# An attention and SwiGLU kernel: the first set's seam in two halves, and a new order of the prologue

## The chip, the cores and the metric

The kernel runs on one core of a Trainium2 chip. The core has TensorE (PE, matmuls into PSUM), VectorE (DVE), ScalarE (ACT), GpSimd (POOL) and SyncE (SP, which issues most DMAs); each works through its own list of instructions in order, and semaphores tie the lists together. The metric is the device time in microseconds (us), as a median of runs.

## The reference

Two blocks follow each other. The first is an attention with 32 inducing points, for 4 batches of 12416 rows of 128 channels: the inducing points attend to the rows, and then the rows to the result h.

```python
def mab(q, kv):
    s = scale * (q @ kv.transpose(0, 2, 1))
    s = s - s.max(-1, keepdims=True)
    a = np.exp(s)
    a /= a.sum(-1, keepdims=True) + 1e-09
    return a @ kv
h = mab(I, x)
return mab(x, h)
```

The second is a feed-forward block on all 49664 rows, with d_ff = 1536:

```python
xn = x / rms * rms_g
g = xn @ w_gate
silu = g * (1.0 / (1.0 + np.exp(-g)))
val = xn @ w_val
return silu * val @ w_out
```

The weights come in as 64-bit numbers, and the kernel makes 32-bit ones of them.

## The kernel before, in words

**Tiling.** A batch's rows are cut into seven sets: five of 2048 rows, one of 1920, one of 256. A set of the large kind has four units (quarters); a unit is 512 tokens wide, and the feed-forward runs for each unit over 12 slots of 128 of the 1536 hidden columns. Since the second attention's output is a combination of the 32 rows of h, the weights w_gate and w_val are multiplied by h once for each batch; the results are the stacks sg and sv. A slot is then a gate matmul (L745) of sg with the unit's moving tile a, SiLU on ScalarE (L753), a value matmul (L756) with sv, their product on DVE (L762), and the matmul with w_out (L682, L703, L705), plain or in three parts for which ScalarE, DVE and POOL prepare factors (L727 to L737). Order and PSUM banks of this long stage stand in lists in the code: which PSUM bank each call takes (`banks`), which work tile (`workers`), at which slot each other step goes (`places`).

**The seam of a set** makes moving tiles out of the second attention's scores. `scores2` multiplies the set's rows, channels first (xT), with h turned over (hT), and DVE turns the result (L440); DVE takes the maximum over the 32 points (L444) and subtracts it (L448), ScalarE takes the exponential (L455). Then `seam` (L499): turn (L511), a matmul with the Gram matrix of h (L515), product and turn (L521, L522), sum and mean square with a floor (L526, L527), the power -1/2 on POOL (L532), its product with the weights (L536), turn (L540), and a split into an upper half of rounded numbers (L548 on DVE for the first set) and the remainder (L549). The normalisation of the softmax falls out, since the RMS norm divides by it again. For the first unit of the first set, `spread` brings upper half and remainder of one quarter to all 128 partitions with two matmuls (L571), and ScalarE copies the result (L574); for the others, `gather` does it with four DMAs from SP (L561).

**The prologue** is everything that comes before the first slot of the first batch: x is loaded (L137, L141), turned by TensorE (L820) and copied by ScalarE and DVE (L826), scored against the inducing points (L341, L832), with maxima by group of sets (L838 to L849), exponentials (L857), turns (L376), sums (L865), sums folded (L400), each group's sum weighed (L878) and turned into hT (L884, L889), and hT is scaled into hg (L425). Beside it the weights are converted chunk by chunk: load (L217), exponent (L257, L237), mantissa (L270, then L239 on ScalarE or L241 on DVE), sign (L279), remainder (L285), product on POOL (L287), and for w_gate and w_val a store to DRAM (L229). A chunk is named by its matrix (0 gate, 1 value, 2 out) and its number: p01 is the exponent of chunk 1 of w_gate. The matmul of a chunk with hg is L483, its copy L484, and L488 takes the remainder for the lower 64 partitions.

**What sets the order.** There is no scheduler: instructions go to the engines in the order in which the code issues them. In the prologue that order is the string ORDER (L793), 170 names that are called one after the other: t transposes, a and v copies by ScalarE and DVE, s scores, m evictions, e exponentials, r turns, h sums, by weighing, p, P, u, U, g, l the weight steps, st and low the stacks, w20 a run of 20 matmuls whose results nobody reads (L191). PSUM banks of the prologue are taken in turn from five (`bank`, L297), work tiles by the digits of `works` (L295). The sequence of SP's DMAs follows from the same order.

Of the kernel before, what the change touches and what calls it, by code (L numbers as in the profile page):

```python
# [18 lines left out]
P = 128  # L19
R = 4  # L20
# [3 lines left out]
def kernel(  # L24
# [269 lines left out]

    NB, turn, turns, works, factors = 5, [0], [], [int(c) for c in "01202121"], []  # L295

    def bank():  # L297
        if turns:
            n = turns.pop(0)
        else:  # L300
            n = turn[0] % NB
            turn[0] += 1
        return ps_gv.tile([P, 512], F32, name="gv", tag=f"gv{n}")
# [5 lines left out]
    def attention(b, load_next):  # L309
# [27 lines left out]
        def scores(s, lhsT, nq, n):  # L337
            w = n * m
            ps = bank()
            for q in range(nq):  # L340
                nc.tensor.matmul(ps[ts(q, m), 0:w], lhsT, xT[b, s][:, ts(q, w)], start=True, stop=True)  # L341
            return ps[0:nq * m, 0:w]
# [94 lines left out]

        def scores2(s, ps=None):
            ps = ps or scores(s, st["hT"][:, 0:m], quarters[s], per2[s])
            nc.vector.transpose(out=sc[b][rows2[s], cols2[s]], in_=ps)  # L440
# [112 lines left out]
    def gather(b, u):  # L553
# [6 lines left out]
        for k, half in enumerate((hi, lo, hi, lo)):  # L560
            nc.sync.dma_start(out=a[ts(k, m), 0:w].bitcast(F32), in_=half[ts(q, m), 0:w].bitcast(F32))  # L561

    def spread(b, u):

        s, q = units[u]
        w = per2[s] * m
        hi, lo = split_of[b, s]
        assert not q and not flowing
        ps = bank()
        for k, half in enumerate((hi, lo)):  # L570
            nc.tensor.matmul(ps[:, 0:w], sel[:, k, :, :].rearrange("p k m -> p (k m)"), half[:, 0:w],  # L571
                             start=not k, stop=bool(k))
        a = moving[b, u] = astk.tile([P, 512], F32R, name="a")
        nc.scalar.copy(out=a[:, 0:w], in_=ps[:, 0:w])  # L574

# [212 lines left out]
    def join(i, c):  # L788
# [4 lines left out]
    ORDER = """  # L793
        open w3 t00 a00 t02 v02 t01 t03 v03 t11 v11 a01 t13 s0 t10 t12 v13 a12 t22 a10 m0 t20 a22 t23 a23 t21 v21 s1
        a20 s2 t30 m1 p00 P00 a30 m2 t31 a31 t33 own0 a33 g00 mB0 nb0 t32 t43 v32 a43 u00 t41 a41 t40 t42 e1 e0 v42 e2
        s3 t51 v40 t50 s4 m3 a50 a51 t53 t52 t60 r0 ls0 h0 r2 U00 r1 l00 a53 a52 a60 s5 m4 own1 m5 s6 mB1 nb1 m6 e3
        own2 p20 e4 h1 u20 r3 mB2 nb2 e6 p10 e5 r4 r6 ls1 ls2 h2 h3 h4 least r5 share shared fold by0 u10 Uv10 h5 h6
        P20 by1 by2 turn_h g20 p01 hT sc2 P10 g10 U20 l10 T2 gram rmax P01 sub exp2 silu l20 ta w11 sq g01 u01 st1 tz
        sum st0 low1 low0 p11 u11 P11 root Uv01 l01 ap tb split w20 spread w3 gather1 gather2 U11
    """  # L800

    def first():
# [87 lines left out]

        def scores2():
            at["scores2"] = f["scores"](0, st["hT"][:, 0:m], R, per2[0])

        def table():
            tiny = small.tile([P, 1], F32, name="tiny")
            S.activation(tiny[:], ones, AF.Silu)

        do = {"open": f["open_"], "least": least_of, "share": shares, "shared": shared,
              "fold": f["fold_l"], "turn_h": turn_h, "hT": copy_h, "sc2": scores2, "gram": f["square_h"],
              "T2": lambda: f["scores2"](0, at["scores2"]), "rmax": lambda: f["row_max"](0), "sub": lambda: f["sub_max"](0),  # L900
              "exp2": lambda: f["exp2"](0, 1), "silu": table, "spread": lambda: spread(0, 0), "lows": lambda: None}
        for n in range(1, 40):
# [18 lines left out]
        for i in range(2):  # L921
            do[f"st{i}"] = lambda i=i: f["stack_of"](i, 0)
            do[f"low{i}"] = lambda i=i: f["stack_low"](i, 0)
        for name, step in zip(("ta", "sq", "tz", "sum", "root", "ap", "tb", "split"), seam(0, 0)):
            do[name] = step
        for u in (1, 2):
# [309 lines left out]
```

## Time and profile before

| | |
|---|---|
| median of 3 runs | 1576.13 us (1575.78 to 1576.47) |
| the profiled execution's own time | 1576.26 us |
| its span, first to last instruction | 1574.4 us |
| granted TensorE clock | 0.999 |
| busy: PE, DVE, ACT, POOL | 1560.7, 1463.9, 1300.1, 1432.8 us |
| first gate matmul (L745) starts | 51.03 us |

The profile is of one execution. Its page shows busy times, the chain of work that ended last, and the costliest groups of instructions. A line of the chain has start, length, engine, what is written and the line. A line of the timeline has start, length, engine, line, operation, tiles and size, and in brackets how long the engine stood idle before it and what ended that. A line of the busy times by stretch has the stretch, its length, the busy us (and instructions) of PE, PE's weight loads, DVE, ACT and POOL, the granted clock, the busy share of the DMA engines and GB/s. A line of the groups by shape has line, engine, operation, tiles, sizes and count, then the sum in us and the mean in ns, and then idle time before.

### The profile page before, as it was taken

How to read it: one execution, taken by the hardware profiler on the slowest of the kernel's cores; microseconds unless marked ns; L12 is line 12 of the kernel's file. 1: busy time of each engine (PE TensorE's matmuls, PEld its weight loads, DVE VectorE, ACT ScalarE, POOL GpSimd, SP SyncE). 2: the span in 40 equal slices, each digit the busy share in tenths (PEclk: the TensorE clock that was granted, in tenths of full speed). 3: DMA queues.
4: the chain of work that ended last, by engine and by line, in shares of the span. 5: the costliest groups of instructions: out<-in, count | busy, mean ns of one | idle time of the engine just before them, and what ended most of it. 6: DMA issues, size and time to landing. Idle time of an engine off the chain costs nothing.

```text
span 1574.4 us, 26146 instructions
## 1 busy us (share of the span) xinstructions
PE 1560.7 (99%) x7152; PEld 1109.1 (70%) x7152; DVE 1463.9 (93%) x2539; ACT 1300.1 (83%) x2496; POOL 1432.8 (91%) x1159
## 2 busy tenths in 40 slices
PE   8999999999999999999999999999999999999998
PEld 6556667767776667776777667776677777777777
DVE  7899999999999998999999999898999999999997
ACT  5677888788888889887988888978798888888886
POOL 1379999999999999999999999899989999999998
PEclk9999999999999999999999999999999999999999
DMA  6445525335453141634444323353222111122221
GB/s 260 104 79 92 100 53 118 79 76 88 68 90 67 33 94 34 134 70 95 71 76 83 54 58 75 73 117 73 47 39 38 37 34 36 33 36 38 40 39 27
DMA packets 389331, 112.58 MB, mean 72 GB/s; under 512 B 365088, under 2 KB 369728, under 8 KB 386624
## 3 DMA queue, kind: packets, MB, share of 16 engines
q1 hardware_dynamic: 388592, 110.83, 35.4%
q8 instruction: 57, 0.93, 0.3%
q14 instruction: 90, 0.74, 0.2%
q10 hardware_dynamic: 592, 0.08, 0.0%
HBM read 53.95 MB, written 27.00 MB: 51 GB/s over the span
## 4 chain that ended last, share of the span: by engine, by line
PE 97%; DVE 2%; DMA 1%; ACT 0%; issue 0%; POOL 0%; SPq 0%; DVEq 0%; ACTq 0%
PE acc L682 32%; PE gv L745 18%; PE gv L756 17%; PE u L703 12%; PE u L705 12%; PE gv L341 3%; PE gv L515 1%; PE gv L390 1%; PE gv L820 1%; DMA xn<-in_x_dram 0%; PE gv L469 0%; DMA a<-lo 0%; PE gv L483 0%; DVE u L762 0%; ACT silu L753 0%
## 5 line engine op out<-in xcount | busy, mean ns | idle before, releaser
L737 POOL TENSOR_TENSOR xn<-xn,xn 128x512 fp32r<-128x512 f32 (+2 forms) x627 | 775.9, 1257 | 47.6 <-DVE xn L728 14.1
L753 ACT ACTIVATE silu<-gv 128x512 f32<-128x512 f32 (+2 forms) x1186 | 683.5, 587 | 136.0 <-PE gv L745 126.0
L756 PE MATMUL gv<-a,sv 128*128 128x512 f32 (+2 forms) x1188 | 566.7, 478 | 0.0
L745 PE MATMUL gv<-a,sg 128*128 128x512 f32 (+2 forms) x1188 | 481.7, 406 | 0.5 <-DMA a<-lo 0.2
L762 DVE TENSOR_TENSOR gv<-silu,gv 128x512 f32<-128x512 f32 (+2 forms) x616 | 412.0, 674 | 34.5 <-PE gv L756 12.5
L762 DVE TENSOR_TENSOR u<-silu,gv 128x512 f32<-128x512 f32 (+2 forms) x570 | 370.1, 656 | 35.4 <-PE gv L756 16.8
L682 PE MATMUL acc<-u,wo 128*128 128x512 f32 (+2 forms) x760 | 369.9, 577 | 0.0
L727 ACT ACTIVATE xn<-gv 128x512 fp32r<-128x512 f32 (+2 forms) x472 | 278.1, 589 | 56.5 <-DVE gv L762 38.5
L728 DVE SCALAR_TENSOR_TENSOR xn<-xn,gv 128x512 fp32r<-128x512 f32 (+2 forms) x472 | 312.5, 662 | 9.4 <-ACT xn L727 4.4
L745 PEld LDWEIGHTS gv<-a,sg 128*128 128x128 f32 x1188 | 223.6, 188 | 132.4 <-issue 32.3
L756 PEld LDWEIGHTS gv<-a,sv 128*128 128x128 f32 x1188 | 223.8, 188 | 106.9 <-issue 26.3
L703 PE MATMUL u<-xn,xn 128*128 128x512 f32 (+2 forms) x600 | 242.8, 405 | 0.0
L682 PE MATMUL acc<-xn,more 128*128 128x512 f32 (+2 forms) x600 | 232.3, 387 | 0.0
L732 POOL TENSOR_TENSOR xn<-u,xn 128x512 fp32r<-128x512 f32 (+2 forms) x155 | 193.1, 1246 | 6.3 <-ACT xn L731 6.2
L682 PEld LDWEIGHTS acc<-u,wo 128*128 128x128 f32 x760 | 142.1, 188 | 43.3 <-issue 17.4
L703 PEld LDWEIGHTS u<-xn,xn 128*128 128x128 f32 x600 | 112.9, 188 | 32.9 <-issue 7.2
L682 PEld LDWEIGHTS acc<-xn,more 128*128 128x128 f32 x600 | 112.7, 188 | 23.5
L737 POOL TENSOR_TENSOR sg<-sg 128x512 fp32r<-128x512 f32 (+2 forms) x97 | 124.5, 1283 | 5.1 <-DVE sg L728 1.9
L737 POOL TENSOR_TENSOR sv<-sv 128x512 fp32r<-128x512 f32 (+1 forms) x96 | 123.1, 1283 | 6.0 <-DVE sv L728 3.0
L705 PE MATMUL u<-xn,more 128*128 128x512 f32 (+2 forms) x305 | 117.6, 386 | 0.0
L705 PE MATMUL u<-xn,xn 128*128 128x512 f32 (+2 forms) x295 | 114.0, 386 | 0.0
L731 ACT ACTIVATE xn<-u 128x512 fp32r<-128x512 f32 (+2 forms) x155 | 95.8, 618 | 12.7 <-DVE u L762 5.8
(216 smaller groups left out, 1920.0 us busy)
## 6 DMA issues: line engine op xcount, KB each, us to landing
out_dram<-o SPq DMA_DIRECT2D x320, 64.0 KB, 2.0
xT<-in_x_dram SPq DMA_DIRECT2D x60, 256.0 KB, 3.8
xn<-in_x_dram SPq DMA_DIRECT2D x60, 256.0 KB, 4.9
a<-hi SPq DMA_DIRECT2D x156, 64.0 KB, 2.0
a<-lo SPq DMA_DIRECT2D x156, 64.0 KB, 2.0
xn<-in_x_dram SPq DMA_DIRECT2D x5, 1024.0 KB, 9.4
xn<-w SPq DMA_DIRECT2D x18, 256.0 KB, 3.1
out_dram<-o SPq DMA_DIRECT2D x64, 60.0 KB, 2.0
```

What stands on the lines that cost most here:

```text
L682: nc.tensor.matmul(acc[:, 0:T], lhsT, rhs, start=st["left"] == NJ, stop=st["left"] == 1)
L703: nc.tensor.matmul(ups[:, 0:T], weight_of(0, j), hi, start=st["k"] == nk, stop=False)
L705: nc.tensor.matmul(ups[:, 0:T], weight_of(1, j), lo, start=False, stop=not st["k"])
L727: nc.scalar.activation(hi, v, AF.Copy, scale=(1.0 - 2.0 ** -13) * 2.0 ** -12)
L728: nc.vector.scalar_tensor_tensor(out=lo, in0=hi.bitcast(F32), scalar=-4096.0, in1=v, op0=ALU.mult, op1=ALU.add)
L731: nc.scalar.activation(d, v, AF.Copy, scale=1.0 - 2.0 ** -13)
L732: nc.gpsimd.tensor_tensor(out=lo, in0=v, in1=d.bitcast(F32), op=ALU.subtract)
L737: nc.gpsimd.tensor_tensor(out=d, in0=hi.bitcast(F32), in1=lo.bitcast(F32), op=ALU.subtract)
L745: nc.tensor.matmul(g[:, 0:T], sg[:, ts(j, P)], a[:, 0:T], start=True, stop=True)
L753: nc.scalar.activation(sl[:, 0:T], g[:, 0:T], AF.Silu)
L756: nc.tensor.matmul(v[:, 0:T], sv[:, ts(j, P)], a[:, 0:T], start=True, stop=True)
L762: nc.vector.tensor_tensor(out=t[:, 0:T], in0=sl[:, 0:T], in1=v[:, 0:T], op=ALU.mult)
```

## The change

The first set's seam is written anew inside `first`, with every step from `scores2` to the copy of the spread cut in two halves of 256 columns (eight of the sixteen groups of 32). Each half is a name of its own in ORDER, with the half's number and a z: sc0z, T0z, rm0z, sub0z and so on to cp1z. The two powers of eight columns follow each other on POOL. The upper halves are copied by ScalarE (`upper`), where DVE did it before. `spread` outside `first` goes away, and `scores2` loses its second argument.

ORDER is a new permutation of the prologue's steps, with the half steps in it. Among the rest: h5 and h6 come before the weighings; Uv10 and Uv01 (L241 on DVE) become U10 and U01 (L239 on ScalarE); the last steps of chunk 01 (low1 g01 U01 l01) come after the two gathers; the runs of unread matmuls w11, w20 and w3 become w7 and w12; sums and copies of the early sets change their order and some their engine. The work tiles' digits change from 01202121 to 01201212. From the first gate matmul on, every engine has the same instructions in the same order as before.

```diff
-    NB, turn, turns, works, factors = 5, [0], [], [int(c) for c in "01202121"], []
+    NB, turn, turns, works, factors = 5, [0], [], [int(c) for c in "01201212"], []
...
     ORDER = """
-        open w3 t00 a00 t02 v02 t01 t03 v03 t11 v11 a01 t13 s0 t10 t12 v13 a12 t22 a10 m0 t20 a22 t23 a23 t21 v21 s1
-        a20 s2 t30 m1 p00 P00 a30 m2 t31 a31 t33 own0 a33 g00 mB0 nb0 t32 t43 v32 a43 u00 t41 a41 t40 t42 e1 e0 v42 e2
-        s3 t51 v40 t50 s4 m3 a50 a51 t53 t52 t60 r0 ls0 h0 r2 U00 r1 l00 a53 a52 a60 s5 m4 own1 m5 s6 mB1 nb1 m6 e3
-        own2 p20 e4 h1 u20 r3 mB2 nb2 e6 p10 e5 r4 r6 ls1 ls2 h2 h3 h4 least r5 share shared fold by0 u10 Uv10 h5 h6
-        P20 by1 by2 turn_h g20 p01 hT sc2 P10 g10 U20 l10 T2 gram rmax P01 sub exp2 silu l20 ta w11 sq g01 u01 st1 tz
-        sum st0 low1 low0 p11 u11 P11 root Uv01 l01 ap tb split w20 spread w3 gather1 gather2 U11
+        open w3 t03 v03 t01 a01 t02 a02 t00 t11 t13 a11 a13 t10 v00 t12 s0 a12 v10 t20 t22 a20 t21 a21 a22 m0 p00 t23
+        a23 s1 m1 t31 s2 m2 t30 P00 a31 t33 own0 a33 t32 g00 mB0 nb0 a30 t41 v41 a32 e2 r2 t40 t43 a40 v43 t50 a50 t42
+        s3 m3 t51 a42 s4 u00 e0 r0 e1 t53 m4 r1 t52 own1 p10 U00 t60 p20 a51 ls0 h0 a52 mB1 l00 a53 a60 s5 nb1 m5 P10
+        s6 e3 h1 m6 own2 mB2 r3 e4 nb2 e6 e5 r4 ls1 least h2 r6 h3 u20 P20 u10 share U10 h4 ls2 r5 shared g10 fold U20
+        p11 l10 h5 h6 by1 by0 by2 g20 turn_h hT sc0z l20 gram T0z sc1z rm0z T1z sub0z ex0z rm1z sub1z ta0z u11 ex1z
+        ta1z silu w7 sq0z zm0z zt0z sm0z mm0z sq1z zm1z st1 zt1z sm1z st0 mm1z rt0z rt1z p01 P11 ap0z low0 U11 tb0z
+        ap1z tb1z hi0z hi1z P01 lo0z w12 sd0z cp0z lo1z sd1z cp1z gather1 gather2 u01 low1 g01 U01 l01
     """
...
+        H, HT = 2, per2[0] // 2
+        def both(k):
+            return slice(k * HT * m, (k + 1) * HT * m), slice(k * HT, (k + 1) * HT)
...
+        def sub_max(k):
+            v = weights(0, 0)[:, both(k)[1], :]
+            V.tensor_tensor(out=v, in0=v, in1=a0["mx"][:, both(k)[1]].unsqueeze(2).to_broadcast((P, HT, m)), op=ALU.subtract)
...
+        def root(k):
+            G.tensor_tensor(out=whole("rs", lambda: small.tile([P, 16], F32, name="rs"))[:, both(k)[1]],
+                            in0=a0["ms"][:, both(k)[1]], in1=mhalf[:, both(k)[1]], op=ALU.pow)
...
+        def upper(k):
+            if not k:
+                split_of[0, 0] = [halves.tile([P, 512], F32R, name=name) for name in ("hi", "lo")]
+            S.copy(out=split_of[0, 0][0][:, both(k)[0]], in_=a0["aT"][:, both(k)[0]])
+
+        def lower(k):
+            hi, lo = (one[:, both(k)[0]] for one in split_of[0, 0])
+            V.tensor_tensor(out=lo, in0=a0["aT"][:, both(k)[0]], in1=hi.bitcast(F32), op=ALU.subtract)
+
+        def spread(k):
+            ps = at["spread", k] = bank()[:, 0:HT * m]
+            for n, half in enumerate(split_of[0, 0]):
+                T.matmul(ps, sel[:, n, :, :].rearrange("p k m -> p (k m)"), half[:, both(k)[0]], start=not n, stop=bool(n))
...
-        for name, step in zip(("ta", "sq", "tz", "sum", "root", "ap", "tb", "split"), seam(0, 0)):
-            do[name] = step
+        for name, step in zip("sc T rm sub ex ta sq zm zt sm mm rt ap tb hi lo sd cp".split(),
+                              (scores2, turn2, row_max, sub_max, exp2, turn_a, square, times, turn_z, total, clamp, root, apply,
+                               turn_b, upper, lower, spread, spread_copy)):
+            for k in range(H):
+                do[f"{name}{k}z"] = lambda k=k, step=step: step(k)
```

## The prediction, on record before the changed kernel ran

> **What bounds the kernel now.** I read the page first. The span is 1574.4 us, and the chain that ended last is 97% TensorE: a long stage that TensorE fills, behind a prologue that it does not fill. The busy time by stretch then shows where the change can act.
>
> ```profile
> span 1574.4 us, 26146 instructions
> ...
> PE 97%; DVE 2%; DMA 1%; ACT 0%; issue 0%; POOL 0%; SPq 0%; DVEq 0%; ACTq 0%
> ```
>
> ```profile
> 36.00:51.00 15.00, 11.42 (x76) 9.13 (x75) 13.24 (x22) 6.09 (x13) 7.01 (x5) 1.00 0.36 110
> 51.00:64.00 13.00, 12.71 (x38) 6.94 (x38) 11.42 (x20) 8.86 (x17) 2.62 (x2) 1.00 0.82 172
> ...
> 130.00:1574.00 1444.00, 1439.07 (x6401) 1031.43 (x6399) 1353.53 (x2322) 1216.44 (x2340) 1372.17 (x1100) 1.00 0.34 65
> ```
>
> From 130 us on TensorE idles 5 of 1444 us: whatever the prologue gives, this stage can only pass on. From 36 to 51 us it is VectorE (DVE, third number) that is nearly full, 13.2 of 15 us, and TensorE's 11.4 us hold filler matmuls (L191) besides. The chain of that stretch lies almost whole on DVE, up to the gather that feeds the second unit:
>
> ```profile
> 34.32 0.20 DVE hT L889
> ...
> 36.35 0.80 DVE hg L425
> ...
> 39.95 1.05 DVE we L279
> ...
> 49.10 0.70 DVE lo L549
> ```
>
> The timeline gives what sits between, and the first gate matmul (L745), from which the long stage counts:
>
> ```profile
> 43.76 2.92 POOL L532 TENSOR_TENSOR rs<-ms,mhalf 128x16 f32<-128x16 f32 x1 [3.31 <-DVE ms L527]
> ...
> 51.03 0.50 PE L745 MATMUL gv<-a,sg 128*128 128x512 f32 x1
> ...
> 52.20 0.69 DVE L762 TENSOR_TENSOR u<-silu,gv 128x512 f32<-128x512 f32 x1 [2.40 <-ACT silu L753]
> ```
>
> The power on POOL takes 2.92 us, four more DVE steps (L536 to L549) follow it one by one, and then DVE itself sits idle for 2.40 us until the first SiLU. A shorter seam and a filled hole are both to be had.
>
> **The change, part by part.** I add up starts by rules that the timeline shows: a DVE instruction starts 0.08 us before its predecessor's end, or 0.03 after it when it reads its result; TensorE starts 0.06 after its producer's end; ScalarE's steps overlap by 0.1. Rows of before in its own order added up so stand 0.15 to 0.2 us early around 50 us, which is the error to expect. Half-size steps have rows of their own, since the kernel's last set is 256 wide:
>
> ```profile
> L762 DVE TENSOR_TENSOR u<-silu,gv 128x512 f32<-128x512 f32 x451 | 301.3, 674 | 29.1 <-PE gv L756 13.8 <-ACT silu L753 10.9 <-ACT xn L727 1.3
> L762 DVE TENSOR_TENSOR u<-silu,gv 128x256 f32<-128x256 f32 x29 | 11.9, 413 | 2.5 <-PE gv L756 1.4 <-ACT xn L736 0.5 <-PE acc L682 0.3
> ...
> L532 POOL TENSOR_TENSOR rs<-ms,mhalf 128x16 f32<-128x16 f32 x20 | 58.0, 2902 | 4.2 <-DVE ms L527 3.5 <-PE gv L756 0.5
> ...
> L532 POOL TENSOR_TENSOR rs<-ms,mhalf 32x8 f32<-32x8 f32 x4 | 6.5, 1626 | 4.2 <-DVE ms L527 4.2
> ```
>
> Two halves of a DVE step cost 2 x 413 - 674 = 152 ns more than one whole. [...] If both halves had to be done before any power began, the gain below would be 1.4 us less.
>
> *Until hT.* The new order moves the sums of sets 5 and 6 ahead, so that the three weighings (L878; before at 30.86, 32.66 and 32.99) run together from 31.85. A product by POOL (L287) then lies at 32.00 to 33.29, and L279 behind the weighings, two SBUF inputs, ends only 0.55 after it, as the row at 39.87 did (1.12 us instead of 0.68, POOL's product ending at 40.45). hT starts at 33.8; before 34.24. Earlier conversions move past each other with the loads arriving as before (the last rows of x at 20.9); I carry 0.3 us of doubt for that.
>
> *hT to the first power.* Before: 34.24 to 43.68, 9.4 us, of which other work on DVE: two L279, two L285, L270, and hg (0.80, held by POOL's product at 35.80; unheld some 0.4, as the three L878 of the same size). After, other work is L285 (0.60), hg (0.32) and L270 (0.34). The seam's steps, start to start: hT 0.20; transpose and maximum of the first half 0.46 and 0.32; second transpose 0.35; subtract, maximum, subtract 0.33, 0.44, 0.33; first turn 0.35; second 0.43; product, turn, sum, mean square 0.45, 0.46, 0.44, 0.16. Sum 6.0: first mean square out at 39.7. The other half's four steps (0.4 each) end at 41.2, beside the first power (to 41.4): hidden, and 0 unless they pass 1.63.
>
> *The powers.* No row has 128x8. From below 1.63 (the 32x8 row; also 2.90 less eight columns of the 0.159 by which the 16-wide row exceeds the 15-wide one, 2.743); from above 2.9, if the width did not matter. I take 1.63. Two end at 43.0, 3.3 us after the mean square; before 43.68 to 46.68, 3.0: 0.3 lost.
>
> *From the last power to the first gate.* Before 46.68 to 51.03, 4.35 us: four whole DVE steps, one of them the upper half (0.77, held by POOL's xn product), then two spread matmuls, ScalarE's copy and fillers. After, one half's worth: apply 0.45, turn 0.43, upper half on ScalarE 0.41, lower 0.45, spread 0.41, copy 0.45: sum 2.6 with the waits between, so the first gate at 45.7. Each half's copy waits on ScalarE; behind it stand the other half and one L237, for which nothing is late. Gain here: 0.4 + 3.5 - 0.3 + 1.7 = 5.3 us.
>
> *What of it is given back.* Chunk w01's L270, L279 and L285, and one L488, now follow the seam: 2.4 us of DVE, with 0.1 more at each change to L488's 64 partitions and back (as at 43.71 and 45.04), in the 2.4 us hole. So that L285 ends at 47.2 and POOL's product xn at 48.5, against 48.59: not earlier at all. The stack matmul L483 that reads it stands in TensorE's order ahead of the fourth gate: it starts at 48.6 instead of 52.80, after an idle 1.2 us. And L279 at 47.7 meets that product and is held to 49.2, 0.86 us that before did not pay; behind it on DVE wait the second u and, through the banks, TensorE. From there DVE's queue runs as before: second u 49.1 (53.40 before), chunk w02's L257 at 56.8 (61.04). Less the 0.15 by which my sums run early: **4.1 us**, kept to the end, because from the first gate on every engine has the same instructions in the same order.
>
> *Moved transfers.* SP's eight gathers (L561, 0.6 us each) now come ahead of the store w01 and the load of the last w_out chunk. They wait for the second upper half, 44.4, on SP's queue; behind them stand store, load and the xT loads. The load starts at 49.5 instead of 49.04 and is read at 65: hidden by 11 us. The second unit's last gather is issued at 46.2; with the 2.0 to 3.0 us of before from issue to landing it is there by 49.2, needed at 49.7. At the 4.1 us that the first one of before took beside the load, it is 0.6 late.
>
> Fillers go from 34 to 19, some 3.5 us of TensorE that nobody waited for. L241 twice goes from DVE to ScalarE (0.42 to 0.63), both under other waits. The three extra bank turns rename banks only.
>
> Sum: 1574.4 - 4.1 = 1570.3 for the profiled execution. Its own time was 1576.26, 1.86 above its span, and 0.13 above the median 1576.13. On the median: **1572.0 us**.
>
> **Rivals.** 0.2% is 3.15 us, about what this kernel's measurement can tell from no change: faster is below 1572.98, slower above 1579.28.
>
> - *Hold of hg*: hg (L425) starts behind L285 while POOL is about to start its wo product (34.7 to 36.0). If POOL comes first, hg waits until 36.0, as at 36.35 above, and the seam moves by 1.0: 1573.0. Against it: L257 at 54.60 stood just so behind L285 with POOL's product at 54.82, and took 0.42.
> - *No give-back*: if L279 is not held by xn and DVE has 0.86 us in hand, the gain is 5.0: 1571.1.
> - *The width does not matter to the power*: twice 2.9 moves the gate by 2.5: 1574.6. The half does not do what it says. The 32x8 row speaks against it.
> - *The long stage gives it back*: a transfer at a fixed time, or POOL at 95% of it, holds the shift: 1574 to 1576. Against it: same order, and loads issued earlier.
> - *Slower: a colder clock.* With fewer fillers TensorE's granted clock could fall. [...] The longest idle before was 1.8 us at a clock of 1.00; after, 1.2 by my sum. [...] It would decide if over 7.3 us of full-speed TensorE work ran at half clock; with all 12.7 us of the stretch behind the gate cold: 1572.0 + 12.7 = 1584.7.
>
> **How the numbers follow.** The forecast's case 0.62 (its own range 1571.1 to 1573.2, from the 0.3 before hT, hg, and the gather); no give-back 0.13; hold of hg 0.10; power 0.05; given back 0.07; clock 0.03. Faster: nine tenths of the first, the second, half of the third: 0.75. Slower 0.03. Same 0.22. The range leaves out the clock, half of what is given back and the power's end: 1570.7 to 1573.9.
>
> **What would show it.** Right: first gate near 45.8, two powers of 1.6, last one ending near 43; hg 0.4 long; xn's product near 47.2; L279 over 1.4 us behind it; the clock at 1.00; every gate after the first dozen 4 us early. Wrong: a power over 2 us, hg near 1.4, a gate waiting for the gather, or a shift at 130 us that differs from that at 62.

## The result, and the profile after

Over 20 runs of each, the changed kernel takes 1574.07 us (1573.51 to 1576.3) and the one before 1576.49 us (1575.75 to 1577.32). The ratio is 0.9985, with a 95% interval of 0.9978 to 0.9992: faster by 2.4 us, and still inside the 0.2% that the prediction called no change. The forecast was 4.1 us, 1572.0 on the median; the time lies 0.2 above the top of the range.

The profiled execution took 1573.86 us, 1.76 above its span. First the page of the changed kernel, its span; then its busy time in one stretch, with the columns of before:

```profile
span 1572.1 us, 26122 instructions
```

```profile
36.00:51.00 15.00, 13.28 (x67) 9.15 (x68) 14.09 (x33) 9.77 (x21) 5.87 (x5) 0.89 0.33 96
```

From 36 to 51 us DVE works 14.1 us instead of 13.2. TensorE's 13.3 us are not more work: the granted clock was 0.89 there, where it had been 1.00. The timeline of the changed kernel has the steps that the prediction gave times to (hT is L877 here, the gate L732, the product u L749):

```profile
34.93 0.29 DVE L877 COPY hT<-gv 128x128 f32<-128x128 f32 x1
...
35.73 0.28 DVE L425 TENSOR_SCALAR hg<-hT,columns 128x128 f32<-128x128 f32 x1
...
41.04 0.17 DVE L931 TENSOR_REDUCE ms<-least 128x8 f32<-128x16 f32 x1
...
41.29 3.27 POOL L935 TENSOR_TENSOR rs<-ms,mhalf 128x8 f32<-128x8 f32 x2 [4.10 <-DVE ms L931]
...
47.30 0.79 PE L732 MATMUL gv<-a,sg 128*128 128x512 f32 x1 [0.46 <-ACT a L962]
...
48.93 1.28 POOL L287 TENSOR_TENSOR xn<-o,we 128x512 f32<-128x512 f32 x1 [4.37 <-PE gv L743]
...
49.43 1.33 DVE L279 SCALAR_TENSOR_TENSOR we<-sv,we 128x512 int32<-128x512 int32 x1
...
50.26 1.33 PE L483 MATMUL gv<-xn,hg 128*128 128x512 f32 x2
...
50.68 0.67 DVE L749 TENSOR_TENSOR u<-silu,gv 128x512 f32<-128x512 f32 x1
```

Two halved powers take 3.27 us, hg is not held (0.28), and L279 is held (1.33). But hT, forecast at 33.8, comes at 34.93, later even than the 34.24 of before. That is 1.13 us of the 1.8 that the span misses of its forecast, the largest part, and what the experiments had to explain.

Where hT's lateness begins can be seen 15 us earlier. In the profile SP issues each of the weight loads below when an earlier load has landed, one by one (0.02 us later: 19.46 and 19.48), so an issue marks a landing. The first load of w_val (sc on L217) marks the landing of the first load of w_gate; the load of w_gate into sg marks that of the first half of x set 5. SP and TensorE of the changed kernel (timeline, one engine each):

```profile
14.48 0.35 SPq L217 DMA_DIRECT2D sc<-in_moe_w_val_dram  x1
...
19.48 0.34 SPq L217 DMA_DIRECT2D sg<-in_moe_w_gate_dram  x1
```

```profile
19.60 1.06 PE L808 MATMUL gv<-ident,xn 128*128 128x128 f32 x8 [0.48 <-DMA xn<-in_x_dram]
```

The same two issues before:

```profile
14.76 0.35 SPq L217 DMA_DIRECT2D sc<-in_moe_w_val_dram  x1
...
18.47 0.34 SPq L217 DMA_DIRECT2D sg<-in_moe_w_gate_dram  x1
```

The half landed 3.71 us after the first w_val load was issued, and now it lands 5.00 us after, with the same loads issued in the same sequence. TensorE waits for it: its transpose behind the wait starts 0.76 us after the one ahead of it, where the others follow each other by 0.11, so 0.65 us are lost.

The shift between the two kernels can be followed by like instructions. It is 2.72 us at L257 of chunk w02 (61.04 before, 58.32 after), 3.09 at the second power (106.71 and 103.62), and 2.22 at the last power (1538.18 and 1535.96); the spans differ by 2.3.

### The profile page after: what moved, and what is told of

The parts are those of the page before. It is cut to its first block, busy times and chain, and to the rows that moved or that the text cites. A ratio compares the mean times of both kernels' runs of the same rounds, so it can differ in the third digit from the quotient of the medians.

```text
span 1572.1 us, 26122 instructions
## 1 busy us (share of the span) xinstructions
PE 1560.3 (99%) x7134; PEld 1107.8 (70%) x7134; DVE 1461.6 (93%) x2544; ACT 1304.9 (83%) x2505; POOL 1432.9 (91%) x1160
## 4 chain that ended last, share of the span: by engine, by line
PE 96%; DVE 1%; DMA 1%; issue 0%; ACT 0%; POOL 0%; SPq 0%; ACTq 0%; DVEq 0%
PE acc L669 31%; PE gv L732 18%; PE gv L743 17%; PE u L690 12%; PE u L692 12%; PE gv L341 3%; PE gv L515 1%; PE gv L390 1%; DMA xn<-in_x_dram 1%; PE gv L469 0%; DVE u L749 0%; PE gv L483 0%; ACT silu L740 0%; PE gv L808 0%; SPq L141 0%
## 5 line engine op out<-in xcount | busy, mean ns | idle before, releaser
L732 PE MATMUL gv<-a,sg 128*128 128x512 f32 (+2 forms) x1188 | 482.6, 407 | 0.7 <-ACT a L962 0.5
L749 DVE TENSOR_TENSOR gv<-silu,gv 128x512 f32<-128x512 f32 (+2 forms) x616 | 412.4, 674 | 34.2 <-PE gv L743 13.4
L749 DVE TENSOR_TENSOR u<-silu,gv 128x512 f32<-128x512 f32 (+2 forms) x570 | 370.7, 657 | 32.8 <-PE gv L743 16.0
L732 PEld LDWEIGHTS gv<-a,sg 128*128 128x128 f32 x1188 | 224.0, 189 | 132.4 <-issue 29.3
L669 PEld LDWEIGHTS acc<-u,wo 128*128 128x128 f32 x760 | 142.2, 188 | 43.3 <-issue 17.4
L718 ACT ACTIVATE xn<-u 128x512 fp32r<-128x512 f32 (+2 forms) x155 | 95.8, 618 | 13.3 <-DVE u L749 6.3
```

Source lines behind the costliest of these rows:

```text
L669: nc.tensor.matmul(acc[:, 0:T], lhsT, rhs, start=st["left"] == NJ, stop=st["left"] == 1)
L718: nc.scalar.activation(d, v, AF.Copy, scale=1.0 - 2.0 ** -13)
L732: nc.tensor.matmul(g[:, 0:T], sg[:, ts(j, P)], a[:, 0:T], start=True, stop=True)
L749: nc.vector.tensor_tensor(out=t[:, 0:T], in0=sl[:, 0:T], in1=v[:, 0:T], op=ALU.mult)
```

## Experiments

All of them compute the whole reference. The theory at the start was: the seam is as short as forecast, and the time missing at the end is lost at hT, through the landing of x. The rivals were that the held L279, the colder clock, or the long stage takes the gain away. In the table, "landing" is from the issue of the first w_val load to the issue of sg's load; the ratio is to the kernel before, run beside it on the same chip (its median was 1576.5 to 1577.5). landing, hT and gate are of one profiled execution each, in us.

| run | median us | less that of before beside it | ratio, 95% | landing | hT | first gate |
|---|---|---|---|---|---|---|
| before | 1576.49 |  |  | 3.71 | 34.24 | 51.03 |
| after | 1574.07 | -2.4 | 0.9985 (0.9978 to 0.9992) | 5.00 | 34.93 | 47.30 |
| sign_late | 1574.90 | -2.6 | 0.9983 (0.9973 to 0.9993) | 5.03 | 35.50 | 47.88 |
| warm_seam | 1573.88 | -3.6 | 0.9979 (0.9970 to 0.9989) | 4.63 | 34.86 | 47.75 |
| upper_dve | 1574.71 | -2.8 | 0.9983 (0.9973 to 0.9992) | 5.29 | 35.78 | 48.59 |
| x_first | 1581.52 | +4.0 | 1.0026 (1.0016 to 1.0035) |  | 42.44 | 54.82 |
| gam_first | 1573.67 | -3.0 | 0.9985 (0.9975 to 0.9994) | 5.12 | 35.57 | 49.76 |
| stack_late | 1574.22 | -2.4 | 0.9984 (0.9974 to 0.9993) | 5.37 | 35.33 | 47.71 |
| whole | 1580.17 | +3.5 | 1.0020 (1.0010 to 1.0029) | 5.28 | 35.36 | 52.50 |
| halves_old_order | 1580.67 | +4.0 | 1.0022 (1.0013 to 1.0032) | 3.64 | 33.97 | 50.37 |
| halves_alone | 1577.72 | +1.2 | 1.0009 (1.0000 to 1.0018) | 3.66 | 33.85 | 52.60 |
| old_head | 1572.12 | -4.4 | 0.9975 (0.9966 to 0.9985) | 3.64 | 33.86 | 46.23 |
| warm_light | 1573.84 | -2.7 | 0.9982 (0.9972 to 0.9991) | 5.27 | 35.26 | 47.65 |
| no_w3 | 1575.58 | -1.4 | 0.9993 (0.9984 to 1.0003) | 3.67 | 35.78 | 48.16 |
| old_head_warm | 1572.44 | -4.5 | 0.9974 (0.9964 to 0.9984) | 3.65 | 34.27 | 46.65 |
| old_head_warm_no_w3 | 1573.51 | -3.4 | 0.9979 (0.9969 to 0.9988) | 3.64 | 34.11 | 46.49 |

### The hold of L279: sign_late

The sign step of chunk w11 (L279 of sv) moves behind the second u.

```diff
-            add(0, weight[1, 1]["sign"])
-            add(1, weight[1, 1]["lower"])
+            add(0, lambda: None)
+            add(1, lambda: (weight[1, 1]["sign"](), weight[1, 1]["lower"]()))
```

> The changed kernel with one step moved: chunk w11's sign step (L279 on sv) goes behind the second unit's first product (the second u) instead of ahead of it. In the changed kernel it ran 49.43 to 50.76, held by POOL's xn product, and the second u began at 50.68 although its SiLU was done at 49.58. Theory (that hold gives back part of the gain): the second u starts at 49.7, L279 behind it takes 0.68, the third u comes at 51.8 instead of 52.2, and the whole is 0.4 to 0.6 us faster than the changed kernel: 1573.5. Rival (the bound behind the first gates is TensorE or the banks, not DVE): the third u stays at 52.2 and the time at 1574.0.

The hold is gone: in sign_late's timeline L279 takes 0.72 us, behind the second u.

```profile
49.40 1.28 DVE L749 TENSOR_TENSOR u<-silu,gv 128x512 f32<-128x512 f32 x2
50.61 0.72 DVE L279 SCALAR_TENSOR_TENSOR we<-sv,we 128x512 int32<-128x512 int32 x1
...
52.18 0.68 DVE L749 TENSOR_TENSOR u<-silu,gv 128x512 f32<-128x512 f32 x1
```

The second u gains, but the third starts at 52.18, 0.04 before the 52.22 of after, with an hT that was 0.57 later. That gain of 0.6 us does not last: from the first gate to the 13th u it is 20.83 us here, and 20.84 in warm_light (below), which has the hold and the same clock. The time is that of after within the intervals. The hold is real and costs next to nothing at the end.

### The colder clock: warm_seam and warm_light

TensorE gets more unread matmuls in the seam.

```diff
-        ... lo0z w12 sd0z cp0z lo1z sd1z cp1z gather1 ...
+        ... lo0z w15 sd0z cp0z w3 lo1z sd1z w4 cp1z gather1 ...   warm_seam
+        ... lo0z w14 sd0z cp0z lo1z sd1z w1 cp1z gather1 ...      warm_light
```

> The changed kernel with ten more filler matmuls in the gaps of TensorE between 44.6 and 47.3 us. Theory A (the clock of 0.50 from 47.35 to 50.7 comes from these gaps, but lies under the hold of L279 and costs nothing): clock 1.00 there, first u about 0.3 us earlier than 48.82, second u at 50.7 as before, time 1574.0. Theory B (the cold clock is what took the missing 1.5 us): the second u comes 1 us or more earlier and the time is 1572.5.

> The changed kernel with three more filler matmuls, in two gaps of TensorE (two ahead of the first spread matmul, one ahead of the first gate), small enough to hold up nothing. Theory (the cold clock that appears behind the seam in some executions costs nothing in most and up to 2 us in few): the median stays the changed kernel's, 2.4 us under the kernel before, within 0.3, with a clock of 1.00 up to 60 us in the profile. Rival (the cold clock costs a part of a microsecond in most): 2.8 to 3.2 us under the kernel before.

The changed kernel's clock fell in the profile. Its busy time in the two stretches on either side of the fall:

```profile
47.30:50.70 3.40, 3.37 (x7) 2.27 (x8) 3.34 (x6) 2.27 (x4) 1.42 (x2) 0.50 0.48 110
43.90:47.31 3.41, 1.99 (x12) 1.21 (x10) 3.15 (x8) 2.13 (x6) 0.66 (x1) 1.00 0.02 5
```

The clock is 0.50 for one stretch of 3.4 us, after one in which TensorE worked 1.99 of 3.41 us; no idle between its matmuls was longer than 0.61 us. With the fillers the clock stays at 1.00 in both runs. In warm_seam they delay the gate by 0.45 us with hT at the place of after, and yet its second u starts at 50.65 against 50.68, and its span is 1572.0 against 1572.1. It gains 3.6 us on the before beside it, warm_light 2.7, both with intervals that overlap that of after. A cleaner measure is the time from the first gate to the second power: 56.32 us in after, and 56.10 to 56.16 in warm_light, sign_late, gam_first, no_w3, old_head_warm and old_head_warm_no_w3, where the clock behind the gate was 1.00 (56.27 in stack_late; 55.68 in warm_seam, whose fillers hold up the gate itself). So the cold stretch costs some 0.2 us in that profile, where it is 3.4 us long and lies where DVE is busy 3.34 of 3.40 us; over many executions it could be up to 1 us, which these runs do not resolve.

The clock isn't always so cheap. The next run was meant for another step, and its profile has a cold stretch of 6.83 us.

### The upper halves back on DVE: upper_dve

```diff
-            S.copy(out=split_of[0, 0][0][:, both(k)[0]], in_=a0["aT"][:, both(k)[0]])
+            V.tensor_copy(out=split_of[0, 0][0][:, both(k)[0]], in_=a0["aT"][:, both(k)[0]])
...
-        ... ap0z low0 U11 tb0z ap1z tb1z hi0z hi1z P01 lo0z ...
+        ... ap0z low0 U11 tb0z hi0z ap1z tb1z lo0z hi1z P01 ...
```

> The changed kernel with the two upper halves made by DVE again instead of ScalarE (the one part undone). DVE gets 0.4 us twice, and loses a wait of 0.17: the first gate 0.6 us later, at 47.9, and the time 0.6 us more than the changed kernel's: 1574.7. Rival (DVE is not what sets the gate; ScalarE's step and its two hand-overs cost as much): no difference, 1574.1.

From hT to the gate it is 12.81 us (35.78 to 48.59), against 12.37 after: ScalarE's copies are worth 0.44. Its median gains as much on the before beside it as after does, so the 0.44 is not resolved in the time. Behind the gate of this profile the clock was 0.50 for 6.83 us, and from L483 to the 13th u it took 20.2 us where runs at 1.00 took 17.9 (from the gate to the second power 58.46 instead of 56.1): a cold stretch of this length behind the gate costs some 2 us.

### What moves the landing: x_first and gam_first

Two runs asked whether other loads push x set 5 back. In x_first the first gate weights wait for a later x set (and p00 stands two sums later); in gam_first the tiny load of the scale, which came behind the four weight loads, goes ahead of them, and each of them waits for one landing more.

```diff
-        for _ in range(1 if s == 3 else 4 if s == NS - 1 else 0):
+        for _ in range(1 if s == 5 else 4 if s == NS - 1 else 0):        x_first
...
+        if s == NS - 1:                                                  gam_first
+            nc.sync.dma_start(out=gam, in_=moe_rms_g.rearrange("(c o) -> c o", o=1))
...
-    nc.sync.dma_start(out=gam, in_=moe_rms_g.rearrange("(c o) -> c o", o=1))
```

> The changed kernel with the first expert weight load (512 KB) put behind all the large x loads in SP's queue, and the step that reads it placed two sums later. Theory (the late landing of x set 5's first half, 19.5 instead of 18.5 us, moved everything up to hT by 1.1 us): that load lands about 1.2 us earlier, hT starts at about 33.8, the first gate at about 46.2, and the time is 1.0 us less than the changed kernel's: 1573.0. Rival (it is not the landing but the order of conversions and scores on TensorE and DVE that makes hT late): hT stays at 34.9 and the time at 1574.0. Slower, if the later weight holds DVE: L257 would stand idle at about 17 us.

> The changed kernel with one tiny load (the 128 scale factors) put ahead of the four expert weight loads in SP's queue, so that each of these is issued one landing later and leaves the x loads more of the DMA engines. Theory (hT follows the landing of x set 5's first half by 15.45 us, as in the four traces 34.93 - 19.48, 35.50 - 20.03, 34.86 - 19.42, 35.78 - 20.33): the half lands 0.5 to 1.0 us earlier against the load that ends before it, hT, first gate and POOL's xn product move by the same, and the time is 0.5 to 1.0 us less than the changed kernel's: 1573.3. Rival: the landing was late because the data came from slower memory and not because of other loads: no change. Slower, if a weight load then comes too late for L257 at 24.6 us.

x_first failed as a test: the first weights landed at 21.1, DVE's L257 waited 3.75 us for them, and hT went to 42.44, so it says nothing of the landing. gam_first is clean for the landing (its later steps are not: its clock was 0.50 for 6.83 us from 34.30, and its gate is late with it). SP of gam_first:

```profile
16.92 0.35 SPq L217 DMA_DIRECT2D sc<-in_moe_w_val_dram  x1
19.60 0.39 SPq L217 DMA_DIRECT2D sc<-in_moe_w_out_dram  x1
20.66 0.34 SPq L217 DMA_DIRECT2D sg<-in_moe_w_gate_dram  x1
```

The first w_val load is issued 2.44 us later than in after, and the half of set 5 (now marked by the second line) still lands at 19.60, which is 5.12 us after the tiny load that took its place at 14.48. The theory that the weight loads compete with x fell.

### Which chain is next: stack_late

The stack matmul L483 of w01 goes two slots later.

```diff
-        0 0 1 1 2 2 2 2 3 3 4 4 ...
+        0 0 1 1 2 2 4 4 3 3 4 4 ...
```

> The changed kernel with one step moved: the stack step of chunk w01 (L483, which reads POOL's xn product) goes two slots later, behind five more gate and value matmuls. Theory (TensorE is full from L483 on, and L483 waits for that product in every trace of the changed seam, at 50.2 us in the changed kernel, so the product sets the shift of the whole long stage): TensorE goes on with gates while it waits, and the time is 0.5 us less than the changed kernel's, 1573.5; up to 0.9 if DVE follows. Rival (DVE, full from 48 to 60 us, sets the shift): no difference, 1574.1.

TensorE no longer waits for POOL's xn, but it doesn't come ahead. Its timeline:

```profile
53.45 1.10 PE L483 MATMUL gv<-xn,hg 128*128 128x512 f32 x2 [0.28 <-DVE u L749]
```

Now it waits for DVE, and the time is that of after. Behind the gate both chains look nearly critical: the wait taken from one only showed the other.

### The halves and the order apart: whole, halves_old_order, halves_alone

```diff
-        H, HT = 2, per2[0] // 2
+        H, HT = 1, per2[0]          whole: one step for both halves, in the new order
```

```diff
-        open w3 t03 v03 t01 a01 ...                                  the new order of ORDER
+        ... rt0z rt1z u01 st1 st0 low1 low0 p11 u11 P11 Uv01 l01 ap0z tb0z ap1z tb1z hi0z hi1z ...   halves_alone
+        ... p11 ap0z tb0z u11 P11 ap1z tb1z ... cp1z w3 Uv01 l01 gather1 gather2 U11                 halves_old_order
```

The last two have all of before's ORDER and its work tiles' digits, with the half steps put in.

> The changed kernel with the seam in one piece of 512 columns again, in the new order and with ScalarE's upper half: the halving alone undone. The steps of the chain at whole size, one behind the other: mean square at about 42.7 instead of 41.04, one power of 2.9 to 45.8, apply, turn, ScalarE's upper half, lower half, spread and copy to a first gate at 49.7 instead of 47.3. Theory (halving is worth 2.4 us at the gate): POOL's xn product, which follows it, comes 1.5 to 2.4 us later and the time is 1575.6 to 1576.5. Rival (the order is what pays, and work from behind the seam fills the hole): within 0.7 us of the changed kernel, under 1574.8.

> The kernel before with the seam in two halves and ScalarE's upper halves, but in its own order of everything else: the halving alone done. Theory: gate at 49.0 to 49.3 instead of 51.03, and nothing taken back since no other work is moved into DVE's hole: 2 us less than the kernel before, 1574.5. Rival (the new order pays): under 1 us less, above 1575.5. On the landing of x set 5's first half: if the order of the prologue decides it, it lands 3.7 us after the load of the first weights, as in the kernel before; if it is chance, anywhere between 3.7 and 5.3.

> As halves_old_order, but with the end of chunk w01 (its number step on DVE, L285 and POOL's product) at its old place ahead of the apply steps, so that the store behind which the gathers queue does not come late: the halving alone, nothing else moved. Theory (without the new order the halves gain little, because other work stands on DVE between the powers and the apply): gate at about 50.4, 0.6 us earlier than before, second unit's gather landed at 54 or later, and a time 0 to 1 us under the kernel before. Rival (the halving is worth its 2 us by itself, and halves_old_order lost them to the gathers only): 2 us under the kernel before.

whole is 3.5 us slower than before where after is 2.4 faster: some 6 us, several times what was expected. Its timeline:

```profile
44.33 0.19 DVE L932 TENSOR_REDUCE ms<-least 128x16 f32<-128x32 f32 x1
44.59 3.03 POOL L936 TENSOR_TENSOR rs<-ms,mhalf 128x16 f32<-128x16 f32 x1 [6.97 <-DVE ms L932]
...
52.50 0.79 PE L732 MATMUL gv<-a,sg 128*128 128x512 f32 x1 [0.68 <-ACT a L963]
```

From hT (35.36) to the mean square it is 8.97 us instead of 6.11 (34.93 to 41.04 in after), and from hT to the gate 17.14 instead of 12.37; its clock was 0.50 for 10 us besides. In halves_alone, where the halves stand in the order of before, the chain does what the halves should do up to the power, and then loses it:

```profile
42.73 0.17 DVE L933 TENSOR_REDUCE ms<-least 128x8 f32<-128x16 f32 x1
42.98 3.27 POOL L937 TENSOR_TENSOR rs<-ms,mhalf 128x8 f32<-128x8 f32 x2 [2.15 <-DVE ms L933]
...
47.23 0.69 DVE L285 SCALAR_TENSOR_TENSOR o<-sg,o 128x512 f32<-128x512 uint32 x1
47.84 0.42 DVE L942 TENSOR_TENSOR sc<-sc,rs 128x256 f32<-128x256 f32 x1
```

The powers end at 46.25, but the first half's apply starts at 47.84, because chunk 01's conversion, issued ahead of it, ends there. The gate comes at 52.60, and the time is 1.2 us above before. halves_old_order moved that conversion behind the spread, but left the gathers behind it; its timeline:

```profile
52.87 0.62 SPq L561 DMA_DIRECT2D a<-hi  x1
...
57.70 0.77 PE L732 MATMUL gv<-a,sg 128*128 128x512 f32 x1 [2.75 <-DMA a<-lo]
```

SP's queue first waits for the store of a product by POOL, so the gathers are issued at 52.87 and TensorE idles 2.75 us. The gate itself came 0.66 earlier than in before. The three runs together: neither part gained time alone. In these profiles the halves lack a DVE cleared behind the powers and an SP cleared ahead of the gathers, which is what the new order gives. How much of each loss is this and how much the clock was not separated: all three profiles have cold stretches, which before has not (whole 3.41 us from 41.29 and 6.83 from 51.53, halves_alone 6.83 from 49.84, halves_old_order 3.41 from 50.64 and from 57.46). In halves_alone the six fillers ahead of the gate took 1.48 us instead of 0.83, so some half of its 1.2 us may be the clock.

### The head: old_head

The changed kernel, with before's order for the first 17 us alone.

```diff
-        open w3 t03 v03 t01 a01 t02 a02 t00 t11 t13 a11 a13 t10 v00 t12 s0 a12 v10 t20 t22 a20 t21 a21 a22 m0 p00 t23
-        a23 s1 m1 t31 s2 m2 t30 P00 a31 t33 own0 a33 t32 g00 mB0 nb0 a30 t41 v41 a32 ...
+        open w3 t00 a00 t02 v02 t01 t03 v03 t11 v11 a01 t13 s0 t10 t12 v13 a12 t22 a10 m0 t20
+        a22 t23 a23 t21 v21 s1 a20 s2 t30 m1 p00 P00 a30 m2 t31 a31 t33 own0 a33 g00 mB0 nb0 t32 t41 v41 a32 ...
```

> The changed kernel with the first third of its order (the transposes, conversions and scores of sets 0 to 3, to about 17 us) as in the kernel before; everything from there on is the changed kernel's. In six traces with the new order x set 5's first half lands 4.6 to 5.4 us after the load of the first expert weights, in two with the old order 3.6 and 3.7. Theory (the order of the first 17 us decides that landing): it lands 3.7 us after, hT comes at 34.0 instead of 34.9, and the time is 0.9 us less than the changed kernel's, 2.4 + 0.9 = 3.3 us under the kernel before. Rival (it is not that part of the order): it lands 4.6 us or more after, and the time is the changed kernel's, 2.4 us under the kernel before.

The fastest median of all, 4.4 us below the before beside it: 6 of its 10 executions took 1571.81 to 1572.15, and none of the 10 of warm_light beside it was under 1573.6 (the intervals of the two ratios overlap). Its timeline:

```profile
18.20 0.34 SPq L217 DMA_DIRECT2D sg<-in_moe_w_gate_dram  x1
...
33.86 0.29 DVE L879 COPY hT<-gv 128x128 f32<-128x128 f32 x1
...
46.23 0.50 PE L732 MATMUL gv<-a,sg 128*128 128x512 f32 x1 [0.46 <-ACT a L964]
```

The half lands 3.64 us after the first w_val load's issue (14.56), and hT is at 33.86, where the forecast had it for the new head. The profiled execution, 1574.19, is one of the slower four: behind the gate the clock was 0.50 for 6.83 us, and from the gate to the second power it took 58.38 us instead of the 56.32 of after.

### What goes with the late landing: no_w3, old_head_warm, old_head_warm_no_w3

In the DMA traffic one packet stands out: the queue that the profile names "instruction" moves 57 packets of 16 KB each in the whole program, and one falls next to the landing of set 5. The DMA view of the changed kernel at 17.4 to 17.6 us (queue and kind; packets, MB, share of the 16 engines):

```profile
q8 instruction: 1, 0.02, 29.3%
```

Its time on a DMA engine is 0.92 to 0.97 us, and 1.00 to 1.33 in the five kernels where it starts latest. The queue of the loads has 97.3% of the 16 engines' time from 17.4 to 18.4 us and the packet 5.9%, together over 100%, so the packet hardly has its engine to itself. Against the issue of the first w_val load, the start of this packet and the landing of the half are, with the load that comes late:

| | packet starts, us after | half lands, us after | late load: us behind the one ahead of it (elsewhere) |
|---|---|---|---|
| whole, warm_seam, warm_light, gam_first, upper_dve, after, sign_late, stack_late | 2.3 to 3.3 | 4.63 to 5.37 | first half of set 5: 2.18 to 2.93 (1.20 to 1.25) |
| before | 3.5 | 3.71 | second half of set 5: 2.44 (0.96 to 1.59) |
| old_head | 3.9 | 3.64 | second half of set 5: 2.28 (0.96 to 1.59) |
| no_w3 | 4.9 | 3.67 | a part of set 6: 1.39 (0.15 to 0.32) |
| old_head_warm, halves_old_order, halves_alone, old_head_warm_no_w3 | 5.5 to 7.3 | 3.64 to 3.66 | first load of w_out: 2.01 to 2.67 (1.22 to 1.34) |

(gam_first is counted from its tiny load. The last column is from the landings in the traces' semaphore records.) x_first, whose loads have another sequence, fits too: the first load of w_gate, 2.33 us behind a half of set 5, is its late one. So in all 16 traces one load that lands 2.0 to 3.6 us after the packet's start is late, and it is another load where the packet lies elsewhere.

The packets come once per 254 to 257 TensorE instructions (matmuls and weight loads, median of each trace), and the count between two packets varies by about 10% for TensorE and by 25% or more for every other engine, so they look like TensorE's own instructions (no view says whose they are). The first of them starts after 218 to 305 of TensorE's instructions, so an order that does more or less on TensorE early should move it against the loads: the author's estimate, which the three last kernels try.

The three last kernels change nothing but the number of unread matmuls: no_w3 is after without the run of unread matmuls at the start, old_head_warm is old_head with warm_light's fillers, and old_head_warm_no_w3 both.

```diff
-        open w3 t03 v03 ...
+        open t03 v03 ...
```

> The changed kernel without the three filler matmuls at the start of its order; nothing else moved. Theory (the refill of TensorE's instructions, 16 KB on one of the DMA engines for 0.94 us, holds up the x load that is just then finishing, and comes when TensorE has used up so many instructions): 12 instructions fewer put the refill about 0.7 us later, at 18.1 to 18.6 us, x set 5's first half lands 3.7 us after the load of the first weights instead of 5.0, hT comes 1 us earlier and the time is 3.3 us under the kernel before instead of 2.4. Rival (the packet is a bystander, or belongs to another engine): packet at 17.4 or the half late all the same, 2.4 us under the kernel before. Slower, if TensorE's clock were cold at the first transposes.

> old_head with warm_light's three filler matmuls in the seam. Theory (the 2 us of 4 in 10 of old_head's executions are the cold clock behind the gate): no execution above 1573, clock 1.00 up to 60 us, 4.5 us under the kernel before. Rival (they come from elsewhere): executions at 1573.3 to 1574.4 as before.

> old_head_warm without the three fillers at the start. Theory of the refill: it moves from 18.4 to about 19.1 us, behind the first half and still ahead of the end of the second, so the second half lands late as in old_head and hT does not move: 4.5 us under the kernel before; if it gets past 19.4 us, both halves are early and hT comes up to 0.5 us earlier. Rival: no relation, any landing.

no_w3 is the test of the two parts of the head, and half of it came out. Its packet starts late (19.92, not the 18.1 to 18.6 of the expectation) and its half lands early, 3.67 us after the first w_val load's issue; its SP:

```profile
15.02 0.35 SPq L217 DMA_DIRECT2D sc<-in_moe_w_val_dram  x1
...
18.69 0.34 SPq L217 DMA_DIRECT2D sg<-in_moe_w_gate_dram  x1
```

The landing goes with the packet, not with the order of the transposes, which is that of after. But in this profile TensorE's clock came up only at 10.04 us (at 4.7 to 7.3 in the others; at 5.33 in old_head_warm_no_w3, which lacks the same matmuls, so their lack alone does not explain it). The timelines of no_w3 and of after:

```profile
6.44 5.45 PE L810 MATMUL gv<-ident,xn 128*128 128x128 f32 x32 [1.25 <-DMA xn<-in_x_dram]
```

```profile
6.32 1.93 PE L808 MATMUL gv<-ident,xn 128*128 128x128 f32 x16
8.43 1.94 PE L808 MATMUL gv<-ident,xn 128*128 128x128 f32 x16 [0.18 <-DMA xn<-in_x_dram]
```

32 transposes took 5.45 us; after did them in two runs of 1.93 and 1.94. So hT came at 35.78, and the interval of the time takes in no change. It doesn't tell what an early landing under the new head is worth. old_head_warm stayed at a clock of 1.00 to near its end, and its span is 1570.6; the forecast said 1570.3. Five of its eight executions took 1572.26 to 1572.49, the other three up to 1573.63, so the clock doesn't explain every slow one. old_head_warm_no_w3 gained nothing at hT and is no faster. The packets of these two also came some 2 and 3 us later than expected (20.50 and 22.12, not 18.4 and about 19.1), so what sets the packet's place to a microsecond is not understood.

## Why the prediction was right or wrong

| step | before | forecast | after | old_head |
|---|---|---|---|---|
| hT starts | 34.24 | 33.8 | 34.93 | 33.86 |
| first mean square out | 43.68 | 39.7 | 41.21 | 40.14 |
| last power ends | 46.68 | 43.0 | 44.56 | 43.48 |
| first gate | 51.03 | 45.7 | 47.30 | 46.23 |
| POOL's xn starts | 47.01 | 47.2 | 48.93 | 47.86 |
| L483 of w01 | 52.80 | 48.6 | 50.26 | 49.19 |
| second u | 53.40 | 49.1 | 50.68 | 49.61 |

**The failed step is "Until hT"**, and in it the clause that the conversions move past each other "with the loads arriving as before", with 0.3 us of doubt. The half of set 5 landed 1.3 us later against the loads ahead of it, and hT came 1.13 late. In seven kernels with the new head (after, sign_late, warm_seam, warm_light, upper_dve, stack_late, whole) hT follows the landing at 15.44 to 15.47 us, whether the landing is 4.63 or 5.37. TensorE lost 0.65 us to it in after, so some 0.65 of the 1.13 is the landing. The other 0.5 or so would be the order of TensorE's work in the new head; it is a remainder, and no run separated it, since no_w3 was spoiled by the clock. old_head gives back both, 1.07. What the step took for given, that unmoved loads arrive as before, did not hold: the 16 KB packet starts 2.0 us ahead of the half's landing in after, 0.2 ahead in before and 0.3 behind in old_head. That the packet delays the load is argued from its coming with a late load in all 16 traces, and no run shows how.

**The seam** held. hT to first mean square took 6.28 us (forecast 5.9), the powers 3.35 from there (3.3), the last power to the gate 2.74 (2.7): 0.47 us of error in 12. The price of half a step, 413 ns from the kernel's own row, was the right one: the seam's steps of 256 columns on DVE took 0.38 to 0.45 each. The power of 128x8 took 1.64 to 1.77, close to the lower of its two bounds, as chosen. With 1.13 for hT, that makes the gate 1.6 late.

**What is given back** went as told. L279 met the xn product and was held to 50.76; L483 waited 0.76 for xn; the second u stands 1.58 behind its forecast, the same 1.6. But the held L279 was the wrong thing to price as the limit: sign_late and stack_late took away one wait each and gained nothing.

**The transfers** were hidden, as forecast: the second unit's last gather was issued at 47.90 and its gate didn't wait for it, where the gate of before had waited 0.20 us for a gather at 54.56.

**The rivals.** The hold of hg, the missing give-back and the power of unchanged price did not come. The colder clock came, though not by a longer idle, by which the prediction had judged it (1.8 us before, at a clock of 1.00, and 1.2 after, by its sum): the clock went to 0.50 after a stretch in which the longest idle was 0.61 us and the work 58% of 3.41 us. The profile of before shows 0.50 only from 1571.89 us on, behind TensorE's last work. No run shows that the longest idle decides it. The forecast adds nothing for the clock, and it cost about 0.2 us in the profiled execution; one execution of 20 (1576.3) may be one with the long cold stretch of upper_dve and old_head; its trace isn't there.

**The long stage** gave back 0.9 us, as that rival said, for no reason that I found. From the second power to the last one it is 1431.47 us before and 1432.34 after, lost in small steps (0.15 by the power at 402 us, 0.57 by that at 784), not in one place. Over all the traces these intervals fall in two groups: 1431.3 to 1431.7 (before, old_head and its two variants, halves_alone, halves_old_order, gam_first, upper_dve) and 1432.1 to 1432.7 (after, sign_late, warm_seam, warm_light, stack_late, whole, no_w3, x_first). All kernels with the old head are in the first group, but two with the new head are too. The cause stays open.

The sum, on the span, forecast 1570.3 and measured 1572.1: 1.52 short at L257 of w02 (hT 1.13, the seam 0.47, less 0.08 won behind the gate), less the 0.15 that was taken off for sums that run early, and 0.40 lost from there to the end, the balance of 0.37 won by 106 us and 0.87 lost in the long stage and 0.09 gained behind it. That is 1.8. The rest of the median's 2.07 lies around the span and in the spread of the runs: 1.76 instead of 1.86 above it, and a profiled execution 0.21 under its median instead of 0.13 over. With the old head and the clock kept warm the span is 1570.6 (old_head_warm), near the forecast, but that does not prove every term: old_head's second u is still 0.5 behind the forecast, and the long stage of that kernel gives nothing back.

## What to carry to other kernels

A sum of steps is worth no more than its start: take the arrival of the data at the head of the chain as an unknown of its own, with its own bounds, when a change touches the order ahead of it, even where not one load is moved. When a chain is shortened, ask which other queue is next by tenths of a microsecond; here the waits of DVE and of TensorE lay so close together behind the gate that undoing one showed nothing in the time. And test parts apart before calling one of them useless or sufficient: the halves lost 1.2 us in the old order, the new order lost 3.5 us without the halves, and together they gained 2.4 (with part of the two losses perhaps the clock's, whose stretches moved too).

## What the runs showed of the hardware that was not expected

**A packet of the "instruction" queue can go with a late load.** In all 16 traces a load that landed 2.0 to 3.6 us after the start of the first 16 KB packet of the "instruction" queue was 0.7 to 1.7 us late; where the packet started 2.3 to 3.3 us after the first w_val load's issue it was the half of set 5, elsewhere another load. no_w3 moved the packet without a change in the order of loads or transposes, and the landing moved with it. The packets go with the count of TensorE's instructions, one per 254 to 257 of them. Not shown is why the delay can be longer than the packet's own time of some 0.95 us.

**TensorE's clock can fall without a long idle.** The cold stretches in the prologue and behind the gate are 3.41 us long, or 6.83. Three of them began after 3.41 us with 1.99 us of TensorE's work (after, old_head) or 2.20 (upper_dve), in after with no idle over 0.61. In after the changes of the clock lie whole multiples of 3.413 us apart: 47.306 and 1569.651 are 446.00 of them apart; in whole 41.29 and 51.53 are 3.00 apart, in halves_old_order 50.64 and 57.46 2.00. Counted so from the rise of before's clock at 5.170 (14 matmuls of 128x128 took 3.35 us ahead of it, 16 took 1.97 behind it), its stretch from 46.13 to 49.54 is one such step; it had 1.62 us of work and an idle of 1.78, and the clock stayed at 1.00. So the share of busy time in such a step does not decide it, and what does stays open.

**A power's price goes with its width.** POOL's power took 1.64 to 1.77 us at 128x8, 2.9 at 128x16, and 1.63 at 32x8: eight columns less save 1.2 us, and 128 partitions instead of 32 cost 0.01 to 0.14.
